# Batch 0's q and k in rows of eight tokens, turned by TensorE; w1 and w2 converted in chunks of 256 rows by 256 columns

## The chip, the cores and the metric

The kernel runs on one core of a Trainium2 chip. The metric is the device time of one execution in microseconds: 1552.49 us before the change (median of three runs, 1552.08 to 1552.88).

A core has five engines with a queue each, which they work off in order: PE (TensorE, matrix products into PSUM), DVE (VectorE), ACT (ScalarE), POOL (GpSimd) and SP (SyncE, which here issues nearly all transfers). L12 is line 12 of the kernel.

## The reference

Pooled attention, a gated MoE layer, and a second one, one after the other:

```python
# attention: B=8, H=8, S=576, D=64, pool=8 -> 72 keys per head
k_p, v_p = (t.reshape(B, H, 72, 8, D).mean(axis=3) for t in (k, v))
attn = softmax(q @ k_p^T / 8)              # 576 x 72 per head
x = (attn @ v_p), heads put together       # 4608 tokens x 512
# MoE, d_ff = 1024
x = ((x @ w1) * (x @ w2) @ w3) @ w_out     # w1, w2: 512 x 1024
# MoE2, d_ff = 2048
h = x @ w_in
out = (h * sigmoid(1.702 * h)) @ w_out2    # 4608 x 512
```

The MoE weights arrive as float64; q, k and v as float32.

## The kernel before

**Precision.** Every large product is the sum of three float32r products (mm3, L113 to L115): each operand is split into a high part (ACT, L103) and a rest (DVE or POOL, L104).

**Converting weights.** The class Conv takes the float64 weights in chunks of 128 x 512. Its `load` (L145) puts a chunk's transfer on SP as soon as a slot of SBUF is free, up to `depth` chunks ahead; its `step` (L154) makes float32 of one chunk (ACT L166 and L167, DVE L168 and L171, POOL L174), turns the one before if it is of w3 (TensorE against the identity, L475), and splits the one before that. The chunks come in a fixed list: 8 of w_out and 16 of w3 in turn, then for each f of 8 a chunk of w1 and one of w2 (128 columns of all 512 rows, `col_tile`), later w_in and w_out2.

**Attention** works on 32 groups of one batch and two heads (n = 4 * batch + head pair). A group's steps are: `g0` turns k and q into columns of head dimension and pools k over eight tokens (kbd, qT); `g1` makes the scores (L271) in the PSUM banks wk[2] and wk[3] and subtracts the maximum (L276, L278); `g2` is the exponential (L286); `g3` the sum and the division (L292 to L295); `g_va` and `g_vb` pool v on POOL; `g4` turns the probabilities, for the first batch (n < NPE) on TensorE through wk[2] and wk[3], else by 20 DVE transposes (L306, issued in `g3`); `g6` makes the output, again in wk[2] and wk[3] (L372 to L375), and splits it into the slots that hold x (L382 on ACT, L383 on DVE). `tick` does a quarter of a group. In `g0` k and q have been loaded in blocks of 32 tokens by 32 dimensions (`load_blocks`, four transfers of 72 KB each, in runs of 128 bytes), so that DVE's 32 x 32 transposes finish the turn (L254, L255); pooling is a sum over eight neighbouring columns (L257).

**The prologue** is a loop of 28 steps of Conv, one tick with each from the fifth on, beside the products of w3 with w_out (`w3_mm`) into the banks acc. It ends with w3 and w_out multiplied into one matrix (wp_s), the first chunks of w1 and w2 converted, and the first 512 tokens of x ready.

**The main loop** goes over 9 blocks of 512 tokens and 8 values of f: x @ w1 and x @ w2 into wk[0] and wk[1] for 128 columns f (24 products each), their product (L602) and its split, one `x2_step` (16 x 3 products with wp_s into acc), two ticks and two steps of Conv. A block of x needs five groups (four and a bit of the next) of attention. MoE2 follows; its first transfers go into five slots (`slota`) that w1's chunks leave in the last block, FA values of f behind.

**What sets the order.** The program is written as straight Python, but the framework's scheduler places each instruction in its engine's queue, by its estimate of when operands and buffers are ready; the order of each engine is fixed then.

Of the kernel before, what the change touches and what calls it, by code (L numbers as in the profile page):

```python
# [17 lines left out]
P = 128  # L18
T = 512
# [3 lines left out]
def pooled_attention_moe_moe2(  # L23
# [32 lines left out]
    NPE = HP  # L56
    SB = S // 32
# [68 lines left out]
    class Conv:  # L126
# [18 lines left out]
        def load(self):  # L145
            while self.todo and len(self.staged) < self.depth and len(free) > self.keep:
                src, turn, done = self.todo.pop(0)
                t = take((P, T, 2), U32)
                d = t.rearrange("p n two -> p (n two)")
                nc.sync.dma_start(  # L150
                    d if len(src.shape) == 2 else d.rearrange("p (c m) -> p c m", c=KM), src)
                self.staged.append((t, turn, done))
# [40 lines left out]
    with pa_ctx:  # L193
# [39 lines left out]
        def g_load(n):  # L233
            if n >= NG:
                return
            b, hp = divmod(n, HP)
            g_k[n] = pa.tile([P, S], F32, name="kr", tag="raw", bufs=4).rearrange("p (g d) -> p g d", d=32)
            load_blocks(g_k[n], k, b, hp)
            g_q[n] = pa.tile([P, S], F32, name="qr", tag="raw", bufs=4).rearrange("p (g d) -> p g d", d=32)
            load_blocks(g_q[n], q, b, hp)  # L240
# [9 lines left out]

        def g0(n):
            kr, qr = g_k.pop(n), g_q.pop(n)
# [8 lines left out]
            g_load(n + 1)  # L261
# [245 lines left out]
        FA = 2  # L507
# [11 lines left out]
        for f in range(NF1):  # L519
            conv.add(col_tile(w1, f), None,  # L520
                     conv.to(w1_s, f, a=f - FA if 0 <= f - FA < NA else None))
            conv.add(col_tile(w2, f), None, conv.to(w2_s, f, nc.vector))

        conv.load()
        g_load(0)
        v_load(0)
        n3 = 8 + 2 * NIT
        done3 = []
        for i in range(n3 + 4):
            key = conv.step()  # L530
            if done3:
                w3_mm(done3.pop(0))
            if key is not None:
                done3.append(key)
            if i >= 4 and tick_n[0] < 20:
                tick()
# [26 lines left out]
        for blk in range(NB):  # L563
# [15 lines left out]
            for f in range(NF1):  # L579
# [3 lines left out]
                for ps, w in ((pa_, w1_s[f]), (pb_, w2_s[f])):  # L583
                    for c in range(KM):
                        mm3(ps, w, sl(c), x[c], slice(0, T), c == 0, c == KM - 1)
                if blk == NB - 1:
                    give(w1_s.pop(f))
                    give(w2_s.pop(f))
# [325 lines left out]
```

## Time and profile before

| | us |
|---|---|
| median of three runs | 1552.49 (1552.08 to 1552.88) |
| the profiled execution | 1552.57 |
| its span, first instruction to last | 1550.9 |
| TensorE busy | 1491.6 (96%) |
| VectorE busy | 983.4 (63%) |
| ScalarE busy | 618.6 (40%) |
| GpSimd busy | 590.1 (38%) |

Busy times are sums over the whole span; which engine sets the pace of a stretch is read from a table of that stretch, and from the waits in it. In the rows below a duration in a row with a count (x5) is that of the whole run of instructions; in the groups by line the figure behind the bar is the busy time in us, then the mean of one in ns, then the idle time ahead of them. A float32 product of TensorE that isn't a transpose (L271) appears as two rows of one line.

### The profile page before, as it was taken

How to read it: one execution, taken by the hardware profiler on the slowest of the kernel's cores; microseconds unless marked ns; L12 is line 12 of the kernel's file. 1: busy time of each engine (PE TensorE's matmuls, PEld its weight loads, DVE VectorE, ACT ScalarE, POOL GpSimd, SP SyncE). 2: the span in 40 equal slices, each digit the busy share in tenths (PEclk: the TensorE clock that was granted, in tenths of full speed). 3: DMA queues.
4: the chain of work that ended last, by engine and by line, in shares of the span. 5: the costliest groups of instructions: out<-in, count | busy, mean ns of one | idle time of the engine just before them, and what ended most of it. 6: DMA issues, size and time to landing. Idle time of an engine off the chain costs nothing.

```text
span 1550.9 us, 19562 instructions
## 1 busy us (share of the span) xinstructions
PE 1491.6 (96%) x6728; PEld 1230.2 (79%) x6728; DVE 983.4 (63%) x1810; ACT 618.6 (40%) x1202; POOL 590.1 (38%) x660
## 2 busy tenths in 40 slices
PE   5975999999999999999999999999999999999998
PEld 4653888888888888887878888888888888888887
DVE  8999988787877877669554244463447253734441
ACT  6774444334344333366553222342225222522231
POOL 7788755555555555359472211101110011101110
PEclk9876999999999999999999999999999999999999
DMA  9971233223232320089879243323343233423310
GB/s 273 248 174 37 57 60 74 54 67 68 59 67 53 74 47 36 27 277 368 347 255 380 89 150 129 128 84 134 111 136 109 102 124 115 150 74 123 129 48 28
DMA packets 225444, 196.33 MB, mean 127 GB/s; under 512 B 158784, under 2 KB 175168, under 8 KB 225344
## 3 DMA queue, kind: packets, MB, share of 16 engines
q1 hardware_dynamic: 224768, 194.03, 40.7%
q8 instruction: 53, 0.87, 0.2%
q10 hardware_dynamic: 576, 1.05, 0.2%
q14 instruction: 47, 0.39, 0.1%
HBM read 150.99 MB, written 44.04 MB: 126 GB/s over the span
## 4 chain that ended last, share of the span: by engine, by line
PE 85%; DVE 8%; DMA 2%; issue 2%; SPq 1%; POOL 1%; ACT 1%; DVEq 0%; POOLq 0%
PE bk L682 22%; PE bk L114 8%; PE bk L115 8%; PE bk L113 8%; PE wk L113 7%; PE wk L115 7%; PE wk L114 7%; PE acc L113 4%; PE acc L115 4%; PE acc L114 4%; PE wk L271 2%; DVE cv L171 1%; DVE s L104 1%; DVE cv L168 1%; DMA s<-in_moe_w_dram 1%
## 5 line engine op out<-in xcount | busy, mean ns | idle before, releaser
L682 PE MATMUL bk<-xM,st 128*128 128x512 f32 x1080 | 261.3, 389 | 0.0
L682 PEld LDWEIGHTS bk<-xM,st 128*128 128x128 f32 x1080 | 202.6, 188 | 42.5 <-ACT o L699 0.4
L113 PE MATMUL wk<-s,s 128*128 128x512 f32 x576 | 228.1, 398 | 6.1 <-ACT s L382 3.7
L114 PE MATMUL wk<-s,s 128*128 128x512 f32 x576 | 226.4, 394 | 4.1 <-DVE s L383 4.1
L115 PE MATMUL wk<-s,s 128*128 128x512 f32 x576 | 225.8, 393 | 1.4 <-DVE s L104 1.4
L114 PE MATMUL bk<-wo,mv 128*128 128x512 f32 x576 | 224.1, 389 | 0.0
L113 PE MATMUL bk<-wo,mv 128*128 128x512 f32 x576 | 223.9, 389 | 0.0
L115 PE MATMUL bk<-wo,mv 128*128 128x512 f32 x576 | 209.9, 389 | 0.0
L306 DVE STREAM_TRANSPOSE p<-s_t 32x160 f32<-32x160 f32 (+1 forms) x560 | 178.6, 319 | 11.0
L818 POOL TENSOR_TENSOR s<-s,sg 128x512 f32<-128x512 f32 x32 | 41.4, 1293 | 332.8 <-ACT sg L817 332.8
L115 PE MATMUL acc<-s,s 128*128 128x512 f32 x352 | 141.0, 401 | 5.1 <-DVE s L104 5.1
L114 PE MATMUL acc<-s,s 128*128 128x512 f32 x352 | 140.0, 398 | 0.4 <-POOL s L104 0.3
L104 POOL TENSOR_TENSOR s<-a,s 128x512 fp32r<-128x512 f32 x56 | 72.7, 1298 | 175.5 <-ACT s L103 135.0
L113 PE MATMUL acc<-s,s 128*128 128x512 f32 x352 | 134.2, 404 | 4.8 <-ACT s L103 4.8
L113 PEld LDWEIGHTS wk<-s,s 128*128 128x128 f32 x576 | 108.5, 189 | 30.6 <-ACT s L382 4.4
L114 PEld LDWEIGHTS wk<-s,s 128*128 128x128 f32 x576 | 109.1, 189 | 27.0 <-DVE s L383 5.3
L115 PEld LDWEIGHTS wk<-s,s 128*128 128x128 f32 x576 | 109.0, 189 | 24.7 <-DVE s L104 1.9
L113 PEld LDWEIGHTS bk<-wo,mv 128*128 128x128 f32 x576 | 108.1, 188 | 22.5
L115 PEld LDWEIGHTS bk<-wo,mv 128*128 128x128 f32 x576 | 108.1, 188 | 22.5
L114 PEld LDWEIGHTS bk<-wo,mv 128*128 128x128 f32 x576 | 108.1, 188 | 22.4
L174 POOL TENSOR_TENSOR cv<-cv,s 128x512 int32<-128x512 int32 x72 | 100.9, 1407 | 56.1 <-DVE cv L171 31.5
L834 DVE TENSOR_TENSOR q<-bk,m 128x512 f32<-128x512 f32 x32 | 22.1, 691 | 150.8 <-PE bk L682 150.8
(152 smaller groups left out, 2548.7 us busy)
## 6 DMA issues: line engine op xcount, KB each, us to landing
st<-wind SPq DMA_DIRECT2D x89, 512.0 KB, 3.4
s<-in_moe_w_dram SPq DMA_DIRECT2D x32, 512.0 KB, 6.7
wind<-s SPq DMA_DIRECT2D x32, 512.0 KB, 5.8
s<-in_moe_w_out_dram SPq DMA_DIRECT2D x24, 512.0 KB, 7.9
s<-wind SPq DMA_DIRECT2D x23, 512.0 KB, 3.4
kr<-in_k_dram SPq DMA_DIRECT2D x128, 72.0 KB, 2.4
qr<-in_q_dram SPq DMA_DIRECT2D x128, 72.0 KB, 2.5
out_dram<-o SPq DMA_DIRECT2D x36, 256.0 KB, 2.0
```

The source lines that it names most:

```text
L104: lo_eng.tensor_tensor(out=dst[:, 1], in0=src, in1=f32(dst[:, 0]), op=ALU.subtract)
L113: nc.tensor.matmul(o, a[:, 0, a_sl], b[:, 0, b_sl], start=first, stop=False)
L114: nc.tensor.matmul(o, a[:, 0, a_sl], b[:, 1, b_sl], start=False, stop=False)
L115: nc.tensor.matmul(o, a[:, 1, a_sl], b[:, 0, b_sl], start=False, stop=last)
L168: nc.vector.tensor_scalar(out=eu, in0=eu, scalar1=4, scalar2=1, op0=ALU.logical_shift_left, op1=ALU.logical_shift_right)
L171: nc.vector.scalar_tensor_tensor(out=wu, in0=hi_w, scalar=0x80000000, in1=eu, op0=ALU.bitwise_and, op1=ALU.bitwise_or)
L174: nc.gpsimd.tensor_tensor(out=w.bitcast(I32), in0=w.bitcast(I32), in1=lo_w.bitcast(I32), op=ALU.add)
L271: nc.tensor.matmul(sc[half][:, i * KW:(i + 1) * KW], qT[:, sl(tt)], mov, start=True, stop=True)
L306: nc.vector.transpose(out=dst[:, :nt, 32 * c:32 * c + 32], in_=s_t[32 * c:32 * c + 32, :nt, 32 * r:32 * r + 32])
L682: nc.tensor.matmul(o, w[:, x, m], b[:, y], start=first and n == 0, stop=last and n == 2, skip_group_check=True)
L818: eng.tensor_tensor(out=v, in0=v, in1=sg, op=ALU.mult)
L834: nc.vector.tensor_tensor(out=q_, in0=o, in1=m1, op=ALU.add)
```

## The change

It does four things.

First, the four groups of batch 0 (n < NS) load k and q differently: one transfer each, [72, 2, 512], a partition holding eight tokens of one head (2 KB in a run), into a slot. `g0_first` then turns them on TensorE: 16 products of k against the identity, in which the eight tokens of a row accumulate, so that pooled k comes out (L267, into wk[2]), and 16 of q, which put every eighth token's column side by side (L275, into wk[2] and wk[3]). ACT copies k from PSUM (L269, L270) and half of q, DVE the other half. From batch 1 on nothing changes there but that k and q are loaded two groups ahead.

Second, w1 and w2 come in chunks of 256 rows by 256 columns (2 KB runs in place of 1 KB). Two chunks serve two values of f. Splits of w1 are on POOL and those of w2 on DVE, as before.

Third, the slots `slota` go to the w1 and w2 chunks of the later f, and FA is 3.

Fourth, the first loads: two chunks, then k and q of group 0, v, k and q of group 1, then the other chunks. The prologue's loop has 30 steps, with ticks from the third on.

```diff
--- before.py
+++ after.py
@@ -54,6 +54,7 @@
     NB = NT // T
     NG = B * HP
     NPE = HP
+    NS = HP
     SB = S // 32
     TT = (S + P - 1) // P
     KW = 2 * SK
@@ -148,7 +149,7 @@
                 t = take((P, T, 2), U32)
                 d = t.rearrange("p n two -> p (n two)")
                 nc.sync.dma_start(
-                    d if len(src.shape) == 2 else d.rearrange("p (c m) -> p c m", c=KM), src)
+                    d if len(src.shape) == 2 else d.rearrange("p (c m) -> p c m", c=src.shape[1]), src)
                 self.staged.append((t, turn, done))
 
         def step(self):
@@ -234,6 +235,13 @@
             if n >= NG:
                 return
             b, hp = divmod(n, HP)
+            if n < NS:
+
+                for g, src in ((g_k, k), (g_q, q)):
+                    g[n] = take(dtype=F32)
+                    nc.sync.dma_start(
+                        g[n][:SK], src[b, 2 * hp:2 * hp + 2].rearrange("h (s u) d -> s h (u d)", u=POOL))
+                return
             g_k[n] = pa.tile([P, S], F32, name="kr", tag="raw", bufs=4).rearrange("p (g d) -> p g d", d=32)
             load_blocks(g_k[n], k, b, hp)
             g_q[n] = pa.tile([P, S], F32, name="qr", tag="raw", bufs=4).rearrange("p (g d) -> p g d", d=32)
@@ -248,7 +256,33 @@
             nc.sync.dma_start(g_v[n], vr[:P])
             nc.sync.dma_start(vtr[:KT], vr[P:])
 
+        def g0_first(n):
+
+            kn, qn = g_k.pop(n), g_q.pop(n)
+            ps = wk[2:]
+            w = POOL // 2 * SK
+            kp = ps[0][:, w:w + SK]
+            for a in range(2):
+                for u in range(POOL):
+                    nc.tensor.matmul(kp[sl(a, D)], kn[:SK, a, sl(u, D)], ident[:SK, :SK],
+                                     start=u == 0, stop=u == POOL - 1)
+            nc.scalar.copy(kbd[:D, 0], kp[:D])
+            nc.scalar.copy(kbd[D:, 1], kp[D:])
+            qv = qT[:, :S].rearrange("p (s u) -> p u s", u=POOL)
+            for h, eng in ((0, nc.vector.tensor_copy), (1, nc.scalar.copy)):
+                for i in range(POOL // 2):
+                    for a in range(2):
+                        nc.tensor.matmul(
+                            ps[h][sl(a, D), sl(i, SK)], qn[:SK, a, sl(POOL // 2 * h + i, D)],
+                            ident[:SK, :SK], start=True, stop=True)
+                eng(qv[:, POOL // 2 * h:POOL // 2 * (h + 1)],
+                    ps[h][:, :w].rearrange("p (u s) -> p u s", s=SK))
+            give(kn, qn)
+            g_load(n + 2)
+
         def g0(n):
+            if n < NS:
+                return g0_first(n)
             kr, qr = g_k.pop(n), g_q.pop(n)
             kT = pa.tile([P, S], F32, name="kT", tag="kT")
             nc.vector.transpose(out=kT, in_=kr.rearrange("p g d -> p (g d)"))
@@ -258,7 +292,7 @@
                 out=ks, in_=kT.rearrange("p (s u) -> p s u", u=POOL), op=ALU.add, axis=AX.X)
             nc.scalar.copy(kbd[:D, 0], ks[:D])
             nc.scalar.copy(kbd[D:, 1], ks[D:])
-            g_load(n + 1)
+            g_load(n + 2)
 
         def g1(n):
             sc = (wk[2], wk[3])
@@ -504,7 +538,7 @@
                         w = wp_s[it] = take()
                         split(w, acc[it % 4], nc.vector)
 
-        FA = 2
+        FA = 3
         n_mm, seen, seen_o = {}, [], []
         for half in range(2):
             for jh in range(2):
@@ -516,23 +550,30 @@
                                          j if j < NA else None))
                     it = half * 4 + i
                     conv.add(w3[sl(it), 2 * jh * T:2 * (jh + 1) * T], w3_turn(it, jh), w3_done(it, jh))
-        for f in range(NF1):
-            conv.add(col_tile(w1, f), None,
-                     conv.to(w1_s, f, a=f - FA if 0 <= f - FA < NA else None))
-            conv.add(col_tile(w2, f), None, conv.to(w2_s, f, nc.vector))
-
+
+        slots_a = list(range(NA))
+        for h in range(NF1 // 2):
+            for w, w_s, eng in ((w1, w1_s, nc.gpsimd), (w2, w2_s, nc.vector)):
+                for c in range(KM // 2):
+                    conv.add(w[sl(c, 2 * P), sl(h, 4 * P)].rearrange("(c p) m -> p c m", p=P), None,
+                             conv.to(w_s, (c, h), eng, a=slots_a.pop(0) if h and slots_a else None))
+
+        conv.depth = 2
         conv.load()
         g_load(0)
         v_load(0)
+        g_load(1)
+        conv.depth = 9
+        conv.load()
         n3 = 8 + 2 * NIT
         done3 = []
-        for i in range(n3 + 4):
+        for i in range(n3 + 6):
             key = conv.step()
             if done3:
                 w3_mm(done3.pop(0))
             if key is not None:
                 done3.append(key)
-            if i >= 4 and tick_n[0] < 20:
+            if i >= 2 and tick_n[0] < 20:
                 tick()
         conv.depth = 8
         give(*(wo_s.pop(j) for j in list(wo_s)))
@@ -580,12 +621,13 @@
                 if conv.busy():
                     conv.step()
                 pa_, pb_ = wk[0], wk[1]
-                for ps, w in ((pa_, w1_s[f]), (pb_, w2_s[f])):
+                h, j = divmod(f, 2)
+                for ps, w_s in ((pa_, w1_s), (pb_, w2_s)):
                     for c in range(KM):
-                        mm3(ps, w, sl(c), x[c], slice(0, T), c == 0, c == KM - 1)
+                        mm3(ps, w_s[c // 2, h], sl(c % 2 * 2 + j), x[c], slice(0, T), c == 0, c == KM - 1)
                 if blk == NB - 1:
-                    give(w1_s.pop(f))
-                    give(w2_s.pop(f))
+                    if j:
+                        give(*(w_s.pop((c, h)) for w_s in (w1_s, w2_s) for c in range(KM // 2)))
                     if 0 <= f - FA < KM:
 
                         t = take_a(f - FA)
```

The order of each engine changes as follows. SyncE's queue at the start, before (s_n are slots, the weights are the float64 inputs), from the sixth transfer on:

```order
L150 DMA s_138<-in_moe_w_dram 128x1024
L150 DMA s_140<-in_moe_w_out_dram 128x1024
L150 DMA s_142<-in_moe_w_dram 128x1024
L150 DMA s_144<-in_moe_w_out_dram 128x1024
L228 DMA kr<-in_k_dram 32x18x32 x4
L228 DMA qr<-in_q_dram 32x18x32 x4
L248 DMA vr<-in_v_dram 128x512
L249 DMA vtr<-in_v_dram 16x512
L150 DMA s_165<-in_moe_w_dram 128x1024
```

and after the change, from the first:

```order
L151 DMA s_128<-in_moe_w_out_dram 128x1024
L151 DMA s_130<-in_moe_w_dram 128x1024
L242 DMA s_132<-in_k_dram 72x2x512
L242 DMA s_134<-in_q_dram 72x2x512
L256 DMA vr<-in_v_dram 128x512
L257 DMA vtr<-in_v_dram 16x512
L242 DMA s_139<-in_k_dram 72x2x512
L242 DMA s_141<-in_q_dram 72x2x512
L151 DMA s_143<-in_moe_w_out_dram 128x1024
L151 DMA s_145<-in_moe_w_dram 128x1024
```

The k, q and v transfers have moved ahead of all but two of the weights, group 1's are among them, and a k or q is one transfer in place of four.

TensorE's queue at the start, before (cv is a converted chunk, acc and wk are PSUM banks, a number behind a name is the buffer):

```order
L475 MATMUL wk_70<-ident,cv 128x128 x4
L113 MATMUL acc_66<-s_185,s_196 128x512
L114 MATMUL acc_66<-s_185,s_196 128x512
L115 MATMUL acc_66<-s_185,s_196 128x512
L475 MATMUL wk_71<-ident,cv 128x128 x4
L113 MATMUL acc_66<-s_211,s_196 128x512
L114 MATMUL acc_66<-s_211,s_196 128x512
L115 MATMUL acc_66<-s_211,s_196 128x512
```

and after:

```order
L267 MATMUL wk_72<-ident,s_132 64x72 x16
L275 MATMUL wk_73<-ident,s_134 64x72 x8
L509 MATMUL wk_70<-ident,cv 128x128 x4
L275 MATMUL wk_72<-ident,s_134 64x72 x8
L114 MATMUL acc_66<-s_183,s_234 128x512
L115 MATMUL acc_66<-s_183,s_234 128x512
L116 MATMUL acc_66<-s_183,s_234 128x512
L305 MATMUL wk_72<-kbd,qT 128x144 x3
L305 MATMUL wk_73<-kbd,qT 128x144 x2
L114 MATMUL acc_66<-s_259,s_234 128x512
L509 MATMUL wk_71<-ident,cv 128x128 x4
L267 MATMUL wk_72<-ident,s_139 64x72 x16
```

Small products of k and q (64x72) and scores now stand between the turned chunks of w3 and the first products with w_out.

VectorE's queue where the fourth head pair's outputs are split into x (s_997 before, s_1045 after: the slot that the first product of the main loop waits for), before:

```order
L292 TENSOR_REDUCE nm<-s_t 128x10
L293 TENSOR_SCALAR nm<-nm 128x10
L294 RECIPROCAL nm<-nm 128x10
L295 TENSOR_TENSOR s_t<-s_t,nm 128x5x144
L306 STREAM_TRANSPOSE p_1076<-s_t 32x5x32 x2
L306 STREAM_TRANSPOSE p_1076<-s_t 32x4x32 x2
L306 STREAM_TRANSPOSE p_1076<-s_t 32x5x32
L383 TENSOR_TENSOR s_997<-wk_72,s_997 128x288
L306 STREAM_TRANSPOSE p_1076<-s_t 32x5x32
L306 STREAM_TRANSPOSE p_1076<-s_t 32x4x32 x2
L383 TENSOR_TENSOR s_997<-wk_73,s_997 128x224
L306 STREAM_TRANSPOSE p_1076<-s_t 32x5x32 x2
L306 STREAM_TRANSPOSE p_1076<-s_t 32x4x32 x2
```

and after:

```order
L326 TENSOR_REDUCE nm<-s_t 128x10
L288 STREAM_TRANSPOSE kT<-kr 128x576
L169 TENSOR_SCALAR cv<-cv 128x512
L417 TENSOR_TENSOR s_1045<-wk_72,s_1045 128x288
L417 TENSOR_TENSOR s_1045<-wk_73,s_1045 128x224
L327 TENSOR_SCALAR nm<-nm 128x10
L169 TENSOR_SCALAR cv<-cv 128x512
L172 SCALAR_TENSOR_TENSOR cv<-s_1270,cv 128x512
L328 RECIPROCAL nm<-nm 128x10
L417 TENSOR_TENSOR s_1054<-wk_73,s_1054 128x64
```

The two splits into that slot, of 128x288 and 128x224, now stand ahead of the fifth group's L295 (L329) and its transposes of probabilities (L306, now L340), and among conversions (L169, L172).

How many instructions stand in VectorE's queue up to and with the second of these splits:

| line before (after) | before | after |
|---|---|---|
| L168 (L169), conversion | 39 | 36 |
| L171 (L172), conversion | 39 | 35 |
| L104 (L105) from a converted chunk | 9 | 8 |
| L254 (L288), k transposed | 8 | 4 |
| L255 (L289), q transposed | 6 | 2 |
| L257 (L291), k pooled | 7 | 3 |
| copy of half of q | 0 | 4 |
| L293, L294 (L327, L328) | 5 each | 4 each |
| L295 (L329), division | 5 | 4 |
| L306 (L340), probabilities | 8 | 0 |

The other lines have as many as before. On POOL, up to its last instruction that this slot waits for (L364, now L398), conversions (L174, now L175) go from 37 to 33 and splits (L104) from 10 to 8, with ten more of the smaller ones that pool v.

## Rows read from the trace of the kernel before

**Rows 1.** The page: 40 slices of 38.8 us (tenths busy), and a transfer's row

```profile
PE   5975999999999999999999999999999999999998
...
GB/s 273 248 174 37 57 60 74 54 67 68 59 67 53 74 47 36 27 277 368 347 255 380 89 150 129 128 84 134 111 136 109 102 124 115 150 74 123 129 48 28
...
s<-wind SPq DMA_DIRECT2D x23, 512.0 KB, 3.4
```

**Rows 2.** Busy time by stage: us, each engine, clock, DMA share, GB/s

```profile
0.00:147.70 147.70, 99.46 (x405) 72.58 (x405) 139.36 (x194) 97.33 (x195) 113.43 (x119) 0.82 0.75 192
147.70:212.20 64.50, 63.02 (x294) 51.93 (x294) 60.26 (x138) 28.97 (x64) 44.23 (x62) 0.98 0.28 54
212.20:300.00 87.80, 87.80 (x427) 74.44 (x426) 69.96 (x174) 34.74 (x78) 47.73 (x70) 1.00 0.27 59
```

**Rows 3.** TensorE in time: start, duration, line, out<-in, [idle before]

```profile
146.26 1.81 PE L271 MATMUL wk<-kbd,qT 128*128 128x144 f32 x6 [5.73 <-DVE s L383]
147.69 0.80 PE L114 MATMUL wk<-s,s 128*128 128x512 f32 x1
```

**Rows 4.** VectorE in time, about 147.7 us and at 212.2 us

```profile
142.36 1.59 DVE L295 TENSOR_TENSOR s_t<-s_t,nm 128x720 f32<-128x720 f32 x1
144.06 1.65 DVE L306 STREAM_TRANSPOSE p<-s_t 32x160 f32<-32x160 f32 x5
...
146.24 0.97 DVE L306 STREAM_TRANSPOSE p<-s_t 32x160 f32<-32x160 f32 x3
147.24 0.39 DVE L383 TENSOR_TENSOR s<-wk,s 128x224 fp32r<-128x224 f32 x1
...
212.18 0.69 DVE L602 TENSOR_TENSOR a<-wk,a 128x512 f32<-128x512 f32 x1
```

**Rows 5.** By line and shape, to 147.7 us: count | busy, mean ns | idle

```profile
L171 DVE SCALAR_TENSOR_TENSOR cv<-s,cv 128x512 uint32<-128x512 uint32 x39 | 40.2, 1039 | 0.3
L168 DVE TENSOR_SCALAR cv<-cv 128x512 uint32<-128x512 uint32 x39 | 34.6, 895 | 4.8 <-ACT cv L166 4.7
...
L104 DVE TENSOR_TENSOR s<-cv,s 128x512 fp32r<-128x512 f32 x9 | 12.9, 1436 | 0.0
...
L271 PE MATMUL wk<-kbd,qT 128*128 128x144 f32 x56 | 12.3, 374 | 7.1 <-DVE s L383 5.7 <-ACT p L354 1.1 <-ACT p L351 0.2
...
L475 PE MATMUL wk<-ident,cv 128*128 128x128 f32 x64 | 12.1, 322 | 10.7 <-POOL cv L174 10.5
...
L295 DVE TENSOR_TENSOR s_t<-s_t,nm 128x720 f32<-128x720 f32 x5 | 6.6, 1321 | 0.0
...
L254 DVE STREAM_TRANSPOSE kT<-kr 128x576 f32<-128x576 f32 x8 | 6.1, 765 | 0.0
...
L257 DVE TENSOR_REDUCE ks<-kT 128x72 f32<-128x576 f32 x7 | 5.2, 737 | 0.0
...
L255 DVE STREAM_TRANSPOSE qT<-qr 128x576 f32<-128x576 f32 x6 | 4.6, 762 | 0.0
...
L372 PE MATMUL wk<-ph,vm 128*128 128x288 f32 x8 | 3.8, 470 | 7.6 <-DVE s_t L278 7.6
...
L278 DVE TENSOR_TENSOR s_t<-wk,nm 128x288 f32<-128x288 f32 x5 | 2.2, 448 | 0.1
```

**Rows 6.** VectorE and POOL in time: long and short forms of one instruction

```profile
8.57 0.41 DVE L168 TENSOR_SCALAR cv<-cv 128x512 uint32<-128x512 uint32 x1
8.78 1.35 POOL L174 TENSOR_TENSOR cv<-cv,s 128x512 int32<-128x512 int32 x1 [0.68 <-DVE cv L171]
9.02 1.67 DVE L171 SCALAR_TENSOR_TENSOR cv<-s,cv 128x512 uint32<-128x512 uint32 x1
10.61 0.68 DVE L104 TENSOR_TENSOR s<-cv,s 128x512 fp32r<-128x512 f32 x1
...
12.75 0.69 DVE L171 SCALAR_TENSOR_TENSOR cv<-s,cv 128x512 uint32<-128x512 uint32 x1
...
46.87 0.89 DVE L295 TENSOR_TENSOR s_t<-s_t,nm 128x720 f32<-128x720 f32 x1
```

## The prediction

> **What bounds the kernel now.** I read the page's slices first: TensorE is full from the fourth slice of 38.8 us on, and only slices 1 to 3 have room [rows 1]. Then the table by stage: up to 147.7 us TensorE is busy 99.5 us and VectorE 139.4 of 147.7; in the next 64.5 us TensorE is busy 63.0; after that it has no idle time, with VectorE at 70.0 of 87.8 [rows 2]. Then TensorE's and VectorE's own rows about 147.7 us. The first full-width MoE product starts at 147.69 (I call this the gate); ahead of it TensorE stood 5.73 us for an L383, and the last L383 that the gate needs starts at 147.24, behind a 1.59 us L295 and eight transposes L306 [rows 3, 4]. So the end of the run is the gate plus a fixed amount of TensorE work, as long as the engines that feed TensorE keep pace after the gate. A change ahead of the gate is worth what it takes from VectorE's queue there, less what is handed back behind it. The profiled execution took 1552.57 us, 1.67 more than its span and 0.08 over the median; I count against 1552.57 and take the median as the same.
>
> **Term 1, the gate.** All of this is VectorE's queue from its first instruction to the fourth head pair's L383 of 128x224; the counts are those of the order. A pooled k and a turned q of four head pairs leave it: 4 × (0.765 + 0.762 + 0.737) = 9.1 us (L254, L255, L257 in [rows 5]). Four copies of half of q come in. Before has no such copy; the nearest row is the L278 of the same 128x288 from PSUM, 0.448 [rows 5], so +1.8. From below it is the 0.39 of the 128x224 L383 [rows 4] (1.6), from above the 0.76 of a whole q transpose (3.0). The eight L306 ahead of the gate fall behind it: 1.65 + 0.97 = 2.6 us [rows 4]. Three L168, four L171, one L104 and one L295 also fall behind it; at their short durations of 0.41, 0.69, 0.68 and 0.89 [rows 6] this is 1.2 + 2.8 + 0.7 + 0.9 = 5.6. But in the prologue they are stretched: means of 0.895, 1.039, 1.436 and 1.321 [rows 5], and a POOL L174 runs 8.78 to 10.13 while an L171 that starts at 9.02 takes 1.67 in place of 0.69 [rows 6]. Over the 92 of them that is 39 × 0.485 + 39 × 0.349 + 9 × 0.756 + 5 × 0.431 = 41.5 us, 0.45 each, so nine fewer take another 4.1. One L293 and L294 less: 0.4. Sum: −9.1 + 1.8 − 2.6 − 5.6 − 4.1 − 0.4 = −20.0.
>
> Against that, the third conversion's load now stands in SyncE's queue behind k, q, both v, and the next k and q. Each of the four k and q transfers moves 72 × 2 × 512 floats, 295 KB; with v the six carry 1.47 MB, at the first slice's 273 GB/s [rows 1] 5.4 us. VectorE has two conversions, about 2 us of stretched work, to put into that time: some +3.5. The DVE account says −16.5 for the gate.
>
> There is a second account. If the stretch is a sharing between VectorE's two-input instructions and POOL, then the sum of POOL's work and VectorE's sharing instructions is what passes, and transposes, the reduction and reads of PSUM cost it nothing: 0.765 and 0.737 in the L254 and L257 show no stretch [rows 5]. In that account only the conversions and splits that fall behind the gate count, four conversions on POOL and the nine on VectorE less some pooling of v that POOL now does sooner: about −8. I take −13 between −8 and −16.5, nearer to the DVE account since the VectorE was busy 94% of the time ahead of the gate and POOL 77% [rows 2].
>
> The Trainium skill has a rule for that stretch ("SBUF — State Buffer", section on SBUF's two separate sides): VectorE and GpSimd share a port pair under an exclusive lock, held for the whole instruction by a VectorE instruction with two SBUF operands. The rows above agree: 1.67 beside a POOL instruction and 0.69 without. By the rule alone the removed transposes were never in the lock and could buy no time; that is the second rival.
>
> **Term 2, what is handed back.** TensorE starts 13 us sooner on a stream of work that VectorE must feed, and the instructions that left the queue ahead of the gate come due behind it. Up to the eighth L602 (212.18, [rows 4]) the order takes only 9.1 − 1.8 = 7.3 us of k and q work out of VectorE's queue; 3.5 of idle time came in. So VectorE can reach that L602 3.8 us sooner by work removed, and 64.5 − 60.3 = 4.2 us sooner by the idle time it now has in that stretch [rows 2]: 8.0 at the most. By the shared account POOL's and VectorE's sharing work up to there is the same as before, and the gain is the idle time less the late start, 4.2 − 3.5 = 0.7. I take 6.5, nearer to the first end since VectorE's row is the fuller one. So of the 13 us, 6.5 are handed back in the 50 to 65 us behind the gate. After it VectorE has 17.8 us of room in 87.8, and nothing more is lost there.
>
> **Term 3, what I cost at nothing or little.** TensorE gets 32 small products for each of four head pairs, 128 in all. They are float32 products like the scores of L271, of which each stands twice in the trace (56 rows for five groups of five and the first three of the sixth, [rows 3, 5]), so 256 rows. From above: six rows of 144 columns run from 146.26 to 147.69 [rows 3], 0.24 each, 61 us. By columns, 72 for 144, 0.12 each, 31 us. From below: once each, and like an L475 of 128 columns at 0.322 [rows 5], cut by columns to 0.18: 23 us. I take 31, the same instruction. All of it lies ahead of the gate, where TensorE has 147.7 − 99.5 = 48.2 us of idle time [rows 2]; a gate that is 13 us sooner leaves 35. So 31 just fits, and at 61 TensorE itself would set the gate, 13 us later than now; this is why I don't take the whole of the DVE account in term 1. ScalarE gets four half-copies, 1.8 us, at 97 of 147.7. SyncE issues 2 transfers a head pair for 8. The w1 and w2 chunks are as many as before, 8 and 8, each with the same conversions; two products of f wait for one pair of row chunks, and two chunks must be there for the first f in place of one: their conversions stand in the queue ahead of the gate's products in both orders. The lookahead FA of 3 frees five slots one step later at the end of MoE; the first loads that use them (3.4 us to landing, [rows 1]) come tens of us before use, and without this cover it would be one landing, 3.4. Below nothing: the prefetch of n + 2 could take a wait out of each group, but no row shows one for k or q.
>
> In sum −13 + 6.5 + 0.5 for the risk in the 3.4 = −6, thus 1552.5 − 6 = 1546.5; its own range 1542 to 1551.
>
> **Rivals.**
> *Nothing handed back.* The instructions moved behind the gate hide in VectorE's waits and TensorE keeps full. For it: TensorE lost only 1.5 us in the 64.5 after the gate [rows 2], so VectorE was not late there. Against it: 4.2 us of room for 9 us of work. It gives 1552.5 − 13 = 1539.5.
>
> *VectorE and POOL share one resource, and it bounds the prologue.* Then POOL plus sharing VectorE work is the same up to the eighth L602, term 2's lower end decides, and the run is 0.7 less at most: 1552. (The Trainium skill's rule above, in "SBUF — State Buffer", is one way to it.) For it: the 41.5 us of stretch. Against: VectorE's transposes stand in an in-order queue with the rest, and while they run POOL has the resource to itself.
>
> *The two PSUM banks of attention.* This one is slower than before. k's and q's turning now writes wk[2] and wk[3], which the scores, the transposes of probabilities and the outputs already pass through, each with a copy out that stands in VectorE's or ScalarE's queue. The group now comes every 23.9 us: the L295 start at 46.87 and, four groups later, at 142.36 [rows 4, 6]. Into this period come 64 rows of 0.12 to 0.24, 7.7 to 15.4 us of TensorE, a copy of 0.45, and a wait behind one stretched conversion of 1.0 for each of the two halves: 10.1 to 17.8 us. Scores take 12.3 us of TensorE up to the gate and the first of four output products 3.8 [rows 5], for five and four groups, so today's use is 2.5 + 4 × 0.9 = 6 plus transposes and copies, perhaps 12 with their waits in queues. With 12 the period would be 22 to 30; with 18 in the banks today, as long as TensorE is behind VectorE's queue, 28 and more. It decides from a period of 23.9 + 13/4 = 27.2 on; at 28.1 the gate is 4 × 4.2 − 13 = 4 us later, and the run 1556.5 with conversions of VectorE waiting behind its copies. For it: TensorE's 5.73 us wait ahead of the gate is a wait in such a bank. Against: both orders put several conversions between two uses of a bank.
>
> **Chances.** Forecast 0.47, nothing handed back 0.20, the sharing 0.17, the banks 0.16. A measurement of this kernel tells 0.2%, 3.1 us, from no change: faster is below 1549.4, slower above 1555.6. Of the forecast's 0.47, 0.41 is below 1549.4; with the first rival 0.61 faster. Same: 0.06 + 0.17 and 0.03 of the banks, 0.26. Slower 0.13. The range runs from 1536 (the DVE account's −16.5 all kept) to 1555.5.
>
> **What would show it.** Right: a first dense product near 134.7; VectorE fuller than 60 of 64.5 in the stretch behind it, with TensorE idle by some 5 to 7 us there; from 215 us on no idle time on TensorE; TensorE's small products at 0.10 to 0.18 apart. Wrong: a gate later than 143 with idle time on VectorE ahead of its copies of q (banks), or near 140 with POOL and VectorE as stretched as now and TensorE waiting behind it for all that it gained (sharing); a gate at 135 and TensorE full at once (nothing handed back). The forecast fails also if conversions wait for loads after the first two, or if MoE2's first products wait for the transfers that FA moves.

## The result: slower, and the profile after

The changed kernel takes 1562.22 us (median of 4 runs, 1561.47 to 1562.65) against 1552.56 for the kernel before on the same chip: ratio 1.0062, 95% interval 1.0045 to 1.0079, some 9.7 us more. The forecast was 1546.5 with a range up to 1555.5.

The first lines are the stages of the changed kernel, in the windows of [rows 2], with the same columns:

```profile
0.00:147.70 147.70, 113.62 (x658) 88.36 (x658) 120.25 (x169) 97.01 (x197) 107.85 (x122) 0.84 0.69 191
147.70:212.20 64.50, 56.00 (x244) 45.14 (x244) 62.97 (x130) 26.14 (x57) 45.39 (x53) 0.92 0.24 45
212.20:300.00 87.80, 87.80 (x426) 74.28 (x425) 72.02 (x176) 35.44 (x81) 45.47 (x65) 1.00 0.30 63
```

Ahead of the old gate VectorE's busy time did fall by 19.1 us, from 139.4 to 120.3, but its idle time rose by as much. Behind the gate it is fuller, and TensorE lost 8.5 us there in place of 1.5. TensorE, about the gate and at the first long wait behind it:

```profile
146.82 1.81 PE L305 MATMUL wk<-kbd,qT 128*128 128x144 f32 x6 [1.28 <-DVE s L417]
148.25 0.80 PE L115 MATMUL wk<-s,s 128*128 128x512 f32 x1
...
162.62 0.80 PE L114 MATMUL wk<-s,s 128*128 128x512 f32 x1 [4.86 <-DVE a L644]
```

The gate comes at 148.25, 0.56 later than in [rows 3]. The wait of 4.86 us at 162.62 is for VectorE, which had the fifth group's twenty transposes of probabilities to do first:

```profile
155.19 6.64 DVE L340 STREAM_TRANSPOSE p<-s_t 32x160 f32<-32x160 f32 x20
161.87 0.69 DVE L644 TENSOR_TENSOR a<-wk,a 128x512 f32<-128x512 f32 x1
```

From the eighth of those products (L602 before, L644 after) to the end nothing differs by much. It starts at 212.18 before [rows 4] and at 222.83 after, and from there to the end of the profiled execution it is 1340.4 us before and 1339.8 after (1552.57 and 1562.65 less these starts). So the loss is made ahead of it, and VectorE's busy and idle time up to it are the account to read. Before, to 212.18, and after, to 222.83 (columns as above; the third busy time is VectorE's):

```profile
0.00:212.18 212.18, 162.46 (x696) 124.49 (x697) 199.60 (x331) 126.30 (x258) 157.66 (x181) 0.87 0.61 150
```

```profile
0.00:222.83 222.83, 180.25 (x953) 142.46 (x954) 193.28 (x322) 127.85 (x262) 158.92 (x181) 0.87 0.54 143
```

VectorE worked 6.3 us less and idled 29.6 us in place of 12.6: −6.3 + 17.0 = +10.7. Two stretches make the idle time. In the first 30 us it is 12.3 in place of 5.3, most of it here:

```profile
15.80 0.43 DVE L169 TENSOR_SCALAR cv<-cv 128x512 uint32<-128x512 uint32 x1 [6.43 <-ACT cv L167]
```

That is the third conversion, whose load now stands behind k, q and v. Between 75 and 125 us it is 14.5 in place of 0.1. That stretch before and after, with the columns of [rows 2]:

```profile
75.00:125.00 50.00, 34.60 (x144) 25.37 (x143) 49.93 (x68) 33.27 (x69) 41.68 (x41) 0.74 0.70 156
```

```profile
75.00:125.00 50.00, 45.82 (x251) 35.80 (x249) 35.45 (x56) 34.16 (x71) 37.03 (x45) 0.86 0.50 140
```

VectorE's waits there after the change (total, times, longest), and the longest of them on three engines:

```profile
DVE s L105 <- ACT s L104: 9.2, 4, 4.1
DVE nm L326 <- ACT s_t L320: 2.7, 1, 2.7
DVE qT L278 <- PE wk L275: 1.5, 1, 1.5
DVE nm L310 <- PE wk L305: 0.7, 1, 0.7
```

```profile
95.36 3.32 PE L267 MATMUL wk<-ident,s 72*64 72x72 f32 x29 [0.70 <-DVE s L417]
```

```profile
99.08 0.21 ACT L269 COPY kbd<-wk 64x72 f32<-64x72 f32 x1 [3.49 <-PE wk L267]
99.30 0.21 ACT L270 COPY kbd<-wk 64x72 f32<-64x72 f32 x1
99.54 0.59 ACT L104 CAST s<-acc 128x512 fp32r<-128x512 f32 x1
```

```profile
95.36 0.72 DVE L172 SCALAR_TENSOR_TENSOR cv<-s,cv 128x512 uint32<-128x512 uint32 x1
100.16 0.69 DVE L105 TENSOR_TENSOR s<-acc,s 128x512 fp32r<-128x512 f32 x1 [4.08 <-ACT s L104]
102.36 0.68 DVE L278 COPY qT<-wk 128x288 f32<-128x288 f32 x1 [1.51 <-PE wk L275]
```

Read them as a chain. L417 takes the last output out of the bank, only then TensorE can turn k of the fourth group into it (95.36); ScalarE stands 3.49 us at the copy of pooled k; the split L104 behind that copy has nothing to do with k, but waits with it, and VectorE 4.08 us with the split. What ScalarE waits for is the turn itself (3.32 us for 29 of its 32 rows); TensorE's wait for the bank was 0.70 and over by then.

This chain and the copy of q account for 4.08 + 1.51 = 5.6 of the 14.5 us. Two others pass through ScalarE as well, but not through a copy of k or q: the 2.74 us of L326 end after ScalarE's wait for a conversion on GpSimd, and the last of L105's waits (1.60) after its wait for turned probabilities (L387):

```profile
90.65 0.62 ACT L104 CAST s<-cv 128x512 fp32r<-128x512 f32 x1 [3.69 <-POOL cv L175]
...
109.32 0.31 ACT L388 COPY p<-wk 32x192 f32<-32x192 f32 x1 [2.21 <-PE wk L387]
```

TensorE was busy 45.8 of these 50 us, where it had 34.6 before, so such a product also stands behind a TensorE that is nearly full.

The division (L329) of the first five groups starts at 34.13, 65.65, 93.57, 129.25 and 152.38 us, 29.6 us a group, against the 23.9 of before (46.87, 70.70, 99.75, 123.23 and 142.36). Two of these rows after the change:

```profile
34.13 0.90 DVE L329 TENSOR_TENSOR s_t<-s_t,nm 128x720 f32<-128x720 f32 x1
...
152.38 2.02 DVE L329 TENSOR_TENSOR s_t<-s_t,nm 128x720 f32<-128x720 f32 x1
```

### The profile page after: what moved, and what is told of

It reads as the page before. It is cut to its first block, busy times and chain, and to the rows that moved or that the text cites. A ratio compares the mean times of both kernels' runs of the same rounds, so it can differ in the third digit from the quotient of the medians.

```text
span 1560.9 us, 20024 instructions
## 1 busy us (share of the span) xinstructions
PE 1509.5 (97%) x6984; PEld 1248.2 (80%) x6984; DVE 978.1 (63%) x1802; ACT 619.8 (40%) x1206; POOL 591.3 (38%) x660
## 3 DMA queue, kind: packets, MB, share of 16 engines
q10 hardware_dynamic: 576, 1.05, 0.2%
## 4 chain that ended last, share of the span: by engine, by line
PE 85%; DVE 8%; DMA 4%; issue 1%; POOL 1%; ACT 1%; SPq 0%; DVEq 0%; POOLq 0%; ACTq 0%
PE bk L724 22%; PE bk L114 8%; PE bk L116 8%; PE bk L115 8%; PE wk L115 7%; PE wk L116 7%; PE wk L114 7%; PE acc L114 4%; PE acc L115 4%; PE acc L116 4%; PE wk L305 2%; DVE cv L172 2%; DVE p L340 1%; DVE s L105 1%; DVE cv L169 1%
## 5 line engine op out<-in xcount | busy, mean ns | idle before, releaser
L340 DVE STREAM_TRANSPOSE p<-s_t 32x160 f32<-32x160 f32 (+1 forms) x560 | 178.5, 319 | 10.6
L105 POOL TENSOR_TENSOR s<-a,s 128x512 fp32r<-128x512 f32 x56 | 72.9, 1302 | 175.2 <-ACT s L104 140.9
L175 POOL TENSOR_TENSOR cv<-cv,s 128x512 int32<-128x512 int32 x72 | 103.1, 1439 | 55.2 <-DVE cv L172 24.0
```

The source lines that it names most:

```text
L105: lo_eng.tensor_tensor(out=dst[:, 1], in0=src, in1=f32(dst[:, 0]), op=ALU.subtract)
L175: nc.gpsimd.tensor_tensor(out=w.bitcast(I32), in0=w.bitcast(I32), in1=lo_w.bitcast(I32), op=ALU.add)
L340: nc.vector.transpose(out=dst[:, :nt, 32 * c:32 * c + 32], in_=s_t[32 * c:32 * c + 32, :nt, 32 * r:32 * r + 32])
```

## The experiments

The kernel before was run beside each group of four or two; its medians were 1552.7 to 1553.0. I counted VectorE's idle time up to the eighth product as above, each from one row of the profile.

**Which part.** Three parts of the change were put back one at a time; the turn was put back on VectorE together with the order of the loads:

```diff
# e1_dve_turn (with the edit of e3):   -NS = HP
                                       +NS = 0
# e2_old_chunks: w1, w2 by col_tile(w, f), main loop on w1_s[f], w2_s[f], FA = 2
# e3_weights_first:  -conv.depth = 2
                      conv.load(); g_load(0); v_load(0); g_load(1)
                     -conv.depth = 9; conv.load()
# e4_ticks:  -if i >= 2 and tick_n[0] < 20:
             +if i >= 4 and tick_n[0] < 20:
```

> The changed kernel with VectorE turning and pooling k and q of batch 0 as before (NS = 0), and the first loads with nine weight chunks first, then k, q, v. It keeps the 256 x 256 chunks, FA, the prefetch and the ticks of the change. To be read against the run in which only the loads' order goes back. Theory W (what VectorE was freed of came back as waiting: the turning through two PSUM banks, with copies in two queues, stretches the period of a group from 23.9 to some 31 us): faster than that run by 3 to 10 us. Theory S (the late first weights alone delay the gate, and the turning is a gain): slower than that run by 5 to 9 us. Theory C (the chunks are at fault): near the changed kernel, 1558 to 1563.

> Only the q and k part of the change: w1 and w2 in the chunks of before (128 columns of all 512 rows), FA = 2, main loop as before; loads, turning and ticks as in the changed kernel. Theory C (four converted chunks are needed for the first f in place of two, so two conversions of some 2.5 us on VectorE stand ahead of the gate or right behind it): faster than the changed kernel by 4 to 8 us, 1554 to 1558. Theories W and S: within 2 us of it, 1560 to 1564.

> The changed kernel, with only the order of the first loads put back: nine weight chunks, then k, q, v of group 0, then k and q of group 1. Theory S (VectorE waited 11.3 us in the first 30 us in place of 4.1, as the third chunk landed at 15.1 us): the gate comes about 7 us sooner, 1554 to 1556. Theories W and C: VectorE's first waits fall to 4 or 5 us, but the group's period sets the gate, and the time stays at 1560 to 1564.

> The changed kernel with ticks of attention from the fifth step of the prologue's loop on, as before, in place of the third. Theory W (the period of a group and not its start decides): the first group comes later and the gate with it by 0 to 8 us, 1562 to 1570. Theory S: the conversions get ahead of the attention again, and the time falls by 2 to 5 us. Theory C: no change within 2 us.

Measured: with VectorE's turn 1549.10 (ratio to before 0.9977, 0.9968 to 0.9987), faster than before; old chunks 1560.09; weights first 1561.37; ticks as before 1558.95. Against the run with weights first, the turning on TensorE costs 12.3 us, a little more than theory W had. The chunks cost little (2.1 us at most; theory C fell). Ticks as before gave 3.3 us, which is what theory S had said and not W. Weights first took 4.3 us out of VectorE's idle time in the first 30 us (8.1 for 12.3), but it came back, the most of it between 75 and 125 us (17.4 for 14.5): theory S fell here, and to the eighth product VectorE's idle time is 29.6 us in both. The row of e1 up to its eighth product at 212.21:

```profile
0.00:212.21 212.21, 158.78 (x696) 123.92 (x697) 196.24 (x330) 125.06 (x258) 158.49 (x181) 0.89 0.59 150
```

Idle 16.0, not 29.6.

**What in the turning.** Four versions, each from the changed kernel:

```diff
# e5_half_products: both heads side by side in the slot (d = 128)
-for a in range(2): matmul(kp[sl(a, D)], kn[:SK, a, sl(u, D)], ident[:SK, :SK], ...)
+matmul(kp, kn[:SK, u], ident[:SK, :SK], ...)            # and the same for q
# e7_other_banks
-ps = wk[2:]
+ps = wk[:2]
# e8_dve_copies: nc.scalar.copy -> nc.vector.tensor_copy for kbd and q's second half
# e6_k_only: q by load_blocks and
+nc.vector.transpose(out=qT[:, :S], in_=qn)
```

> The changed kernel with half as many products: both heads of a pair side by side in a slot (four transfers a group for two, runs of 256 bytes), so that one product of 72 x 128 against the identity turns what took two of 72 x 64: 16 a group for 32. Theory P (TensorE's time in the turning, 64 rows of 0.105 us a group at the low clock, stands in the chain of a group): 3.3 us a group less, 1549 to 1556. Theory B (that the turning has to pass the two PSUM banks of attention, however long it takes) and theory A (that its copies stand in ScalarE's queue ahead of splits for which VectorE waits): 1559 to 1564.

> The changed kernel with the turning in wk[0] and wk[1], through which w3's chunks are turned, in place of wk[2] and wk[3]. Theory B (the wait for a bank that L417 or the scores still hold): k and q are turned ahead of their group, the period falls towards 24 to 27 us, 1548 to 1555. Theories P and A: the products and the copies are the same, 1558 to 1564.

> The changed kernel with all four copies out of PSUM (two of pooled k, two halves of q) on VectorE, none on ScalarE. Theory A (ScalarE's queue waits at these copies for TensorE, and the splits behind them hold VectorE, 9.2 us of VectorE's waits between 75 and 125 us): 1553 to 1558. Theories P and B: no gain, 1560 to 1566, since VectorE has four times 0.9 us more to do ahead of the gate.

> The changed kernel with only k turned and pooled by TensorE; batch 0's q is loaded in blocks and turned by VectorE as before. It takes away half of the products, the two copies of q and the use of the second bank. Theory P: half of the cost of turning goes, 1554 to 1558. Theory B: one wait for a bank a group is left in place of two or three, 1553 to 1558. Theory A: two of four copies are left on ScalarE, those at which it waited longest (3.5 us), 1558 to 1562.

Measured: half the products 1559.28; other banks 1552.59; copies on VectorE 1562.72; k alone 1549.88 (0.9979, 0.9970 to 0.9989). In the other banks the turning writes over chunks of w3 that wait there, so a part of w3's product is made of other numbers; the instructions are the same. The copies' engine doesn't matter (theory A fell). Half the products gave 2.9 us, less than theory P had. k alone came out below all three theories. Out of attention's banks, all of the loss is gone, as theory B had said; the first four divisions come 19.9 to 24.8 us apart, the fifth 35.6 us after the fourth, 25.4 a group.

**The other half, and the banks without the overwriting.**

```diff
# e9_q_only: k by load_blocks, transpose and reduce on VectorE as before
# e10_free_bank: turned = banks with a turned chunk of w3 not yet split
-ps = wk[2:]
+bank = wk[1] if 0 in turned else wk[0]
+ps = (bank, bank)
# e11_free_bank_wf = e10 + the edit of e3;  e12_k_only_wf = e6 + the edit of e3
```

> The changed kernel with only q turned by TensorE; batch 0's k is loaded in blocks, turned and pooled by VectorE as before. The other half of the run in which only k was turned (1549.9). If it is q's two stays in wk[2] and wk[3] that hold the groups up (theory B): 1559 to 1564. If any turning of half the size is free, and only both together are too much for the chain: 1549 to 1555.

> The changed kernel with k and q turned in that one of wk[0] and wk[1] which holds no turned chunk of w3 at the time, both halves of q one after the other; nothing else changes. Theory B: the period of a group falls from 31.7 to under 27 us and VectorE's waits between 75 and 125 us from 14 to under 5 us: 1549 to 1555. If what helped in the two other banks was something else (that run overwrote turned chunks of w3, and so had other dependences): 1557 to 1563.

> As the run with the free bank, and the nine weight chunks load first again. Theory S, now that the banks no longer hide it: VectorE waits 7 us less in the first 30 us, and 3 to 7 us of it reach the end, 1544 to 1550. Rival: what the conversions gain at the start stands behind the gate anyway, within 2 us of the free bank's time.

> Only k turned by TensorE, and the nine weight chunks load first again. Theory S: 2 to 5 us less than with k alone turned and the changed loads (1549.9): 1545 to 1548. Rival: k's transfer, now behind 4.7 MB of weights, holds up the first group and the time stays within 1.5 us of 1549.9.

Measured: q alone 1549.68 (0.9980, 0.9970 to 0.9989), the free bank 1552.40, the free bank with weights first 1557.83, k alone with weights first 1550.03. The free bank takes 9.8 us off with every product, copy and transfer of the change in place; VectorE's waits between 75 and 125 us in it are these, 6.3 us where theory B had said under 5, and its row to the eighth product is below them:

```profile
DVE cv L169 <- ACT cv L167: 4.5, 1, 4.5
DVE s L105 <- ACT s L104: 1.8, 2, 1.1
```

```profile
0.00:215.72 215.72, 175.63 (x965) 140.43 (x966) 191.19 (x319) 127.41 (x262) 158.10 (x181) 0.93 0.56 146
```

Of VectorE's 29.6 us of idle time 24.5 are left, so the free bank takes away the waits of one stretch and not the most of them. TensorE is as full there as in the changed kernel (44.7 of the 50 us), so that a full TensorE alone does not make these waits. It looks as if the passage through attention's two banks were a part of the loss. But q alone passes both banks too and loses nothing (theory B had 1559 to 1564 for it), and weights first made the free bank 5.4 us slower, which neither theory had. With k alone weights first changed nothing, as the rival had said.

**Is it the length of the stay?**

```diff
# e13_q_twice (from e9)                     # e14_k_twice (from e6)
-for a in range(2):                         -for u in range(POOL):
+for a in (0, 1, 0, 1):                     +for u in (*range(POOL), *range(POOL)):
# e15_loads_only: VectorE's turn, and g_load also loads k and q into two slots, read by nothing
# e16_q_half_products: e9 with the slot and products of e5 for q
```

> Only q turned by TensorE (1549.7), with every product of the turning issued twice into the same place: 64 rows a group, as long on TensorE as k and q together in the changed kernel, with half of its copies and slots. If the length of the stay in wk[2] and wk[3] holds the groups up: 1555 to 1562, VectorE's waits between 75 and 125 us back at 10 us or more. If it is the number of copies and of hand-overs between queues, or of slots: 1548 to 1552.

> Only k turned and pooled by TensorE (1549.9), with every product issued twice, the second round starting the sum anew. Length of the stay: 1554 to 1561. Number of hand-overs or slots: 1548 to 1552. A result between (1552 to 1554): each of the two has a share.

> VectorE turns k and q as before; the changed kernel's loads of k and q into slots are made as well and read by nothing (the kernel does this in excess of the work), with the load order and chunks of the change. If slots and transfers for both k and q hold the conversions up: 1555 to 1562. If the turning alone costs: near the run in which VectorE turned (1549.1), with up to 3 us for the late first weights, 1548 to 1553.

> Only q turned by TensorE, with one product for both heads: 8 a group in place of 16. If the stay in the banks no longer sets the pace with q alone: 1548 to 1551, as with 16. If its length still counts, half of it gives 2 to 3 us: 1546 to 1548.

Measured: q twice 1557.06 (7.4 more than once; its ten runs went from 1554.25 to 1562.07), k twice 1561.07 (11.2 more), loads only 1565.66, q with half the products 1560.64, 11.0 us more than with all of them. The times of the first two fit the length of the stay, though VectorE's idle time between 75 and 125 us was 5.3 with q twice (in the profiled run, the fastest of the ten), where 10 or more had been expected. The last contradicts it: a quarter of the changed kernel's products, and 7.7 us over the kernel before. It loads q in two transfers of 256-byte runs for one of 2 KB, which is not separated from the products. Its VectorE idles 24.7 us to the eighth product, with q alone 17.5. The profiles of e9 and e16 to that point:

```profile
0.00:210.88 210.88, 165.45 (x827) 130.16 (x828) 193.43 (x329) 126.67 (x262) 162.04 (x181) 0.87 0.61 150
```

```profile
0.00:221.24 221.24, 169.41 (x760) 136.44 (x761) 196.59 (x331) 126.65 (x262) 157.68 (x181) 0.85 0.59 144
```

The loads alone lost by another way: idle time is only 18.2, but VectorE is busy 207.8 us up to the eighth product:

```profile
0.00:225.97 225.97, 164.39 (x697) 125.92 (x697) 207.81 (x328) 124.89 (x258) 158.51 (x181) 0.89 0.63 151
```

That is 11.6 us more than in e1 in two instructions fewer, the same ones with longer means: 0.97 us for 0.82 in L169, 1.70 for 1.04 in the division, 1.52 for 1.20 in the splits of a converted chunk. So this kernel, which turns nothing on TensorE, loses more than the changed one. A different order stands behind each of these kernels, as the scheduler places the whole queue anew for each edit, and the last two runs were made for that.

**The same instructions in another order.**

```diff
# e17_q_before_k: the lines of g0_first that turn q moved ahead of those that turn k
# e20_other_order
-with _tile.TileContext(nc, schedule_with_timeline_sim=True) as tc:
+with _tile.TileContext(nc, schedule_with_timeline_sim=False) as tc:
```

> The changed kernel with the lines that turn q written ahead of those that turn k: the same instructions, tiles and banks, another order in the queues. Theory O (the time that was lost is the order's, which stands instructions that wait for a bank or a copy ahead of others that could run): the time moves by over 3 us, to 1549 to 1558 (or above 1565). Theory W (the work of turning both in these banks costs what was measured): 1559 to 1565.

> The changed kernel with the scheduler's other mode (schedule_with_timeline_sim off), which places the same instructions by priority and not by estimated times. Theory O: the time moves by over 3 us either way; VectorE's waits up to 215 us differ from the changed kernel's 29 us by as much as the time does. Theory W: 1559 to 1565, with VectorE's waits near 29 us.

Measured: q before k 1559.55, 2.7 less than the changed kernel; the other mode 1611.17, 48.9 more, and VectorE idle 62.9 us to its eighth product at 249.55:

```profile
0.00:249.55 249.55, 186.05 (x962) 146.52 (x963) 186.61 (x320) 128.79 (x263) 149.54 (x167) 0.86 0.43 121
```

Of the 48.9 us, 26.7 lie ahead of the eighth product (in the profiled run; its idle time is 33.4 us longer, its work 6.7 shorter) and some 21 behind it, where theory O had put all of it into the waits. The order can cost far more than the change did; a small change of order, on the other hand, left the loss where it was, within the bounds that I had given for theory W.

All runs side by side: in the scheduler's first mode, the seven kernels in which both k and q pass attention's banks, each in an order of its own, took 1558.95 to 1562.72 us. The four with the change's chunks and prefetch in which neither does, and no transfer is added, took 1549.10 to 1557.83. That speaks for the banks. It isn't proof: edits that leave the banks alone, or ease them, moved the time by 5.4 us (weights first with the free bank), 11.0 (q with half the products) and 16.6 (loads only, in the change's order, against VectorE's turn), as much as the loss and more.

## Why the prediction was wrong, point by point

**Term 1 failed**, by what it left out. Its count of VectorE's work was right: −20.0 forecast for the queue up to the fourth head pair's split of 128x224, −19.7 measured to that split's end (139.3 us before, 119.6 after). The sum is closer than its parts: a copy of half of q took 0.70 us where 0.45 was written, and the conversions, their splits and the division are 11.9 us less where 9.7 was written. But I took the queue for full, so that work removed is time gained, and allowed 3.5 us of new idle time. It was 19.1: 7.0 at the start, where I had written 3.5 (two conversions take 3.9 us at the stretched means, not the 2 that I set against the transfers), and 14.5 between 75 and 125 us, where I had written none; other stretches gave a little back. The gate moved by +0.56 in place of −13. That the time went idle is shown; what made each wait of the 14.5 us is shown only in part.

**The rival of the two banks came nearest, but its account didn't hold.** It had the direction, a gate later than 143 us and idle time on VectorE. Ahead of the copies of q, where it had put this idle time, there was 1.5 us. It was to decide from a period of 27.2 us on; the period was 29.6, and by its sum, 4 × 5.7 − 13, the gate would have come 9.8 us later. It came 0.56 later: the first group's division stood 12.7 us sooner, and the fifth's no longer stands ahead of the gate; the loss appeared behind it. Nor does the period order the runs: it is 26.1 us with weights first (1561.37), 27.7 with k alone (1549.88) and 21.0 in the other mode (1611.17). For the banks speaks that the free bank takes back 9.8 us. That one wait spreads through ScalarE's queue to VectorE is read from the rows above, and moving the copies did not help. What stays open is why k alone (in wk[2]) and q alone (in both) pass these banks at no loss while q with fewer products loses 11.0: the order differs in each, and no run kept the changed kernel's order while a duration in it changed. So the banks are likely a cause of the loss; that they are the cause, and not the order that came with them, is not shown.

**Term 2 was right in kind and too small.** The stretch from the gate to the eighth product grew from 64.5 us to 222.83 − 148.25 = 74.6, 10.1 more where I had written 6.5; VectorE's work in it rose from 60.3 to 193.3 − 120.8 = 72.5. The work is handed back although the gate has not come sooner. I had tied it to a gate that moves; the work left the queue ahead of the gate by the order, and comes due by the order.

**Term 3 erred to the safe side on the products.** They take about 20 us in all, where 31 was written and 23 as the bound from below, added up from their rows, which stand 0.05 to 0.11 us apart. Two runs of 16 rows each:

```profile
28.95 1.23 PE L275 MATMUL wk<-ident,s 72*64 72x72 f32 x16
...
35.20 0.72 PE L275 MATMUL wk<-ident,s 72*64 72x72 f32 x16
```

What I took from it was wrong: that 31 us fit into 48 of idle time says nothing of when the bank is free and which engine stands behind the copy. The copy of half of q took 0.70 in the mean in place of 0.448, 1.0 us in all.

**The chunks and FA** cost 2.1 us at the most (e2), where nothing was written.

**Nothing handed back** fell with the rows at 155 to 163 us. **One resource of VectorE and POOL**: the stretch stayed (a conversion's L172 has a mean of 1.05 us ahead of the gate, where L171 had 1.04 in [rows 5]), but the end came from waiting, which that rival did not have.

**A reading of the page** was off by one: the fourth digit of TensorE's row in [rows 1] is 5, and TensorE is full from the fifth slice on. No sum uses it.

Four versions beat the kernel before by 0.2%: VectorE's turn with the new chunks (1549.10), k or q alone on TensorE (1549.88 and 1549.68), and k alone with weights first (1550.03). Their intervals overlap, so none is shown to be the best.

## What to carry to other kernels

An engine that is 94% busy is a bound only as long as nothing that it waits for gets longer: before taking work from its queue, follow the new path of the data (which bank, which copy, what stands behind the copy in that engine's queue), and ask what else will wait there. Where a scheduler places the whole program anew for each edit, work moved out of a stretch by the order comes due in the next, and the account is to be made up to the point where the queue of work is the same again; here it is the eighth product, from which on the kernels before and after differ by 0.6 us (all kernels but the one in the other mode took 1336.0 to 1340.8 from there, a spread that is itself half of the loss). With such a scheduler one edit that gains or loses 10 us does not name a cause, since edits that add or take little work moved the time as far. An edit that saves work is tried alone and in halves, since two that are each harmless were not together.

## What the runs showed of the hardware

The third weight chunk was issued at 4.75 us, behind the transfers of k, q and v, and was landed at 15.09, after the 10.34 us that the chain of waits shows for it; VectorE stood idle for 6.43 us, until the conversion's step on ScalarE was done as well (15.80). I had put 5.4 us for the transfers and two conversions to cover a part.

The products of the turning depend on TensorE's clock more than I had allowed. The table of stages at two runs of 16 rows (L275) has the granted clock in the last column but two: 0.50 of full (the lower of its two levels, 1.2 GHz) in the first and 1.00 (2.4 GHz) in the second.

```profile
29.00:30.10 1.10, 1.10 (x17) 0.96 (x16) 1.10 (x1) 0.64 (x1) 1.08 (x1) 0.50 0.85 251
35.20:35.90 0.70, 0.70 (x18) 0.62 (x17) 0.43 (x1) 0.17 (x1) 0.70 (x1) 1.00 1.09 234
```

The 16 rows took 1.23 us at the first and 0.72 at the second, and the fourth group's k was turned at 0.50 (95.40 to 98.30 us), the third's at 1.00 in 2.02 us for 32 rows where the fourth's had 3.32 for 29. Ahead of 35.20 us TensorE had worked without a gap from 23.87 on; ahead of the fourth group's k it was busy for 2.3 of the 5.0 us from 90.40 on. The first group's k does not fit: its first 29 rows took 3.29 us, as long as at 0.50, and the table shows 1.00 for 8.30 to 9.90 us. Why, no run here shows.

```profile
8.27 3.29 PE L267 MATMUL wk<-ident,s 72*64 72x72 f32 x29 [8.27 <-DMA s<-in_k_dram]
8.30:9.90 1.60, 1.60 (x15) 1.60 (x17) 1.07 (x2) 0.12 (x1) 0.99 (x1) 1.00 1.05 251
```
